# Twelve attention outputs transposed by VectorE squares and a DRAM trip in place of TensorE, with decays scanned in place

## The chip, the cores and the metric

The kernel runs on one core of a Trainium2 chip. The metric is the device time in microseconds (us) of one execution, taken as a median over runs. The engines of the core are named as the profile names them: PE is TensorE (PEld is its weight load), DVE is VectorE, ACT is ScalarE, POOL is GpSimd, and SP is the engine whose queue issues nearly all DMAs here.

## The reference, cut to what matters

A gated linear attention (4 batches, 8 heads, 768 positions, head size 40) is followed by two feed-forward layers over its 3072 tokens of width 320, each with 2048 hidden units. All data is 32-bit float.

```python
# attention, per batch and head, over positions t
C = f_stab * C + i_stab * outer(v_t, k_t);  n = f_stab * n + i_stab * k_t
y[:, :, t] = sigmoid(o_gate_t) * (C @ q_t) / max(abs(n @ q_t), 1)
# then, with the heads side by side as x of [3072, 320]
h = x @ w_in;   x = (h - tanh(h)) @ w_out                 # layer 0
h = x @ w2_in;  g = h if h >= 1, 0 if h <= -1, else (h + 1)**2 / 4
out = g @ w2_out                                          # layer 1
```

## The kernel before, in words

**Tokens and blocks.** The positions of each batch are cut in 6 chunks of 128. One chunk of one batch, with all its 8 heads, is a *job*; there are 24, numbered 0 to 23 (job n is chunk n // 4 of batch n % 4). Four jobs make a *block* of 512 tokens. Layer 0 of block k needs the attention outputs of its four jobs, 4k to 4k + 3.

**Steps.** Each layer goes over 6 blocks of 16 *steps*. A step of layer 0 takes 128 of the 2048 hidden units: 8 matmuls of 512 columns into a PSUM bank `h` (`step`, line 650), then on ACT a tanh (line 668) and a rounded copy `gh` (line 681), on DVE a subtraction (line 669) and the rest `gl` (line 682), and two steps later 12 matmuls of 320 columns into the four `a` banks (`second`, line 702). Two `h` banks are in turn. From block 2 on the steps go in pairs: 16 matmuls of line 650, then 24 of line 702. After 16 steps `evac` has VectorE turn the four `a` banks in squares of 32 by 32 (line 713) and stores them to DRAM (`xr_d`), from where layer 1 loads them in place.

**Jobs beside steps.** The jobs of block k + 1 run while layer 0 of block k runs. A job loads its inputs; scans the decays on DVE (line 460, `fb` in, `d` out); forms the scores on PE (lines 473 and 489), multiplies them into `d` on DVE (line 493), and sums on PE into the bank `t_n`: from the state `C` (line 520), and from scores and values (line 529). Then come a denominator (lines 536 to 539) and the output gate `o3`, a part of the tile `nat`. Line 546 (DVE) multiplies `t_n` and `o3` into the tile `x`, with 128 tokens on the partitions and 320 features along them. Layer 0 wants it the other way round: line 551 has PE transpose `x` in three pieces into a PSUM bank `t_x`, and `split_x` (lines 597 to 607) writes from that bank a rounded part (ACT) and the rest (DVE) into the `x1` tile of the block, which the matmuls of line 650 read. The state is renewed by matmuls of line 558, five copies on ACT and three updates on DVE (line 575).

**What sets the order.** The whole program is first recorded: `op` notes an operation with its engine, an assumed duration and a due time in steps (`prio`). `schedule` then places operations by due time and readiness, and `issue` writes the instructions of each engine in that order. On the chip each engine works strictly in order, and so does SP's queue: a DMA whose wait is not over holds up all behind it. A job of block k ≥ 1 gets its due times from line 816: 6 steps (`AHEAD`) before its share of the block before, its loads 3 steps earlier still. At every chunk the gates (`gates`, `decays`) of all batches are computed, which takes exponentials (line 365) and then sigmoids (line 504) on ACT, with a table load for each. `background` converts a weight tile of layer 1 every four steps and stores it to DRAM (`w_d`). Buffer numbers are the last argument of `abuf`: before, `fb` has 2 and `d` has 3.

Of the kernel before, what the change touches and what calls it, by code (L numbers as in the profile page):

```python
# [7 lines left out]
F32 = mybir.dt.float32  # L8
# [6 lines left out]
ALU = mybir.AluOpType  # L15
PSUM = bass.MemoryType.PSUM

B, H, S, D = 4, 8, 768, 40
L = 128
NC = S // L  # L20
DM = H * D
DF = 2048
NF = DF // 128
# [3 lines left out]
HU = H // 2  # L27
# [5 lines left out]
BLK = [4, 4, 4, 4, 4, 4]  # L33
NB = len(BLK)
BLK0 = [sum(BLK[:j]) for j in range(NB)]
NJ = B * NC
# [9 lines left out]
AHEAD, LOADS = 6, 3  # L46
# [7 lines left out]
W_AHEAD = 5  # L54
FFN = 4
STACK = 12
GS = 4
HTAGS = ["h", "h", "tn", "tb"]

# [16 lines left out]
class Plan:  # L76
# [20 lines left out]
    def op(self, eng, ns, prio, fn, r=(), w=(), out=None, lock=False):  # L97
        o = Op()
        o.eng, o.ns, o.prio, o.fn, o.seq, o.out = eng, ns, prio, fn, len(self.ops), out
        o.allocs, o.preds, o.succs = [], set(), []  # L100
        o.bufs, o.fill, o.lock = [], 0, lock
        key = lambda x: x if isinstance(x, tuple) else (x, None)

        for x in map(key, r):
            if x in self.last:
                o.preds.add(self.last[x])
            self.read.setdefault(x, []).append(o)
        for x in map(key, w):
            if x in self.last:
                o.preds.add(self.last[x])  # L110
            o.preds.update(self.read.pop(x, ()))
            self.last[x] = o
        o.preds.discard(o)
        for b in {key(x)[0] for x in (*r, *w)}:
            if isinstance(b, Buf):
                b.users.append(o)
                o.bufs.append(b)
        if any(b.place[0].startswith("late_") for b in o.bufs):
            o.preds.add(self.gate)
        self.ops.append(o)  # L120
        return o
# [92 lines left out]
def dve(n):  # L214
    return 157 + n / 0.96
# [16 lines left out]
def mlstm_moe_moe(ctx: ExitStack, tc: tile.TileContext, ig, fg, qk, qk3, q3, nat, w1, w2, cst, out):  # L232
    nc = tc.nc
# [5 lines left out]
    dram = ctx.enter_context(tc.tile_pool(name="dram", bufs=1, space=bass.MemoryType.DRAM))  # L239
# [11 lines left out]
    gr_d = dram.tile([B * H, S], F32, name="gr_d")  # L251
    w2_d = dram.tile([NF, 128, WC], F32, name="w2_d")
    xr_d = dram.tile([DM, NT], F32, name="xr_d")

    att = ExitStack()
    ap = att.enter_context(tc.tile_pool(name="ap", bufs=1))
# [10 lines left out]
    def abuf(tag, shape, dtype, cap, name=None):  # L267
        att_tags.add(tag)
        return P.buf(of(ap), shape, dtype, tag, name or tag, cap)
# [12 lines left out]
    def load(prio, dst, src, kb, r=(), w=(), rows=None, eng="SP"):  # L282

        size = rows or 4096
        ns = kb * 1024 / size / 16 * (8 + size / 18.0)
        op(eng, 0, prio, lambda: (nc.sync if eng == "SP" else nc.scalar).dma_start(out=dst(), in_=src()), r, w, out=ns)
# [108 lines left out]
    def jbank(n, what, name):  # L395

        tag = {"s0": "tn", "s1": "tb", "n": "tn", "x": "tn", "c": "tb", "f": "h"}[what]
        if n < FIRST and what in "s0s1xc":
            tag = (("a3", "tb"), ("a0", "a1"))[n % 2][what in ("s1", "x")]
        return bank(tag, name)  # L400
# [5 lines left out]
    def job(n, at, ld):  # L406
# [15 lines left out]
        f = {}  # L422
        if n >= FIRST:
            for u in range(2):
                ft = abuf("fb", [128, HU, L], F32, 2)
                load(ld + 0.5, lambda ft=ft: ft.t, lambda u=u: fr_d[
                    b * H + u * HU:b * H + (u + 1) * HU, c * L:(c + 1) * L].unsqueeze(0).to_broadcast([128, HU, L]),
                    256, r=[("fr_d", kc)], w=[ft], rows=512)
                f[u] = lambda ft=ft: ft.t.rearrange("p h t -> p (h t)"), ft
# [15 lines left out]
        for u in range(2):  # L445
            p = at(0) if u == 0 else at(1)
            if n < FIRST:
                ft = jbank(n, "f", "t_f")
                for h in range(HU):
                    r = b * H + u * HU + h  # L450
                    op("PE", 2 * pe(L, 128, 2), p, lambda h=h, r=r, ft=ft: nc.tensor.matmul(  # L451
                        ft[:, h * L:(h + 1) * L], ident[:, r:r + 1].to_broadcast([128, 128]),
                        gt[0][0][:, 0:L], start=True, stop=True), [gt[0][0], (gt[0][0], "z", 32), (gt[0][0], "z", 64), "cs"], [ft])
                f[u] = lambda ft=ft: ft.t, ft
            if d0 is None:
                d = abuf("d", [128, 512], F32, 3)
                dk[u] = lambda d=d: d.t, d
            else:
                dk[u] = lambda u=u: d0[:, u * 512:(u + 1) * 512], (d0, u)
            op("DVE", dve(1024), p, lambda o=dk[u][0], i=f[u][0]: nc.vector.tensor_tensor_scan(  # L460
                out=o(), data0=i(), data1=scan_id, initial=0.0, op0=ALU.mult, op1=ALU.add), [f[u][1], "scan_id"], [dk[u][1]], lock=n >= FIRST)
            if not last:
                op("ACT", 200, p + 0.3, lambda u=u, i=dk[u][0]: nc.scalar.copy(  # L463
                    wc[:, u * HU:(u + 1) * HU], i().rearrange("p (h t) -> p h t", t=L)[:, :, L - 1]), [dk[u][1]], [(wc, u)])
# [77 lines left out]
        if not xt:  # L542
            xt.append(abuf("x", [128, 384], F32, 1))
            op("POOL", 170, -80, lambda: nc.gpsimd.memset(xt[0][:, DM:384], 0.0), [], [(xt[0], "z")])
        x = xt[0]
        op("DVE", dve(DM), at(6), lambda: nc.vector.tensor_tensor(
            out=x[:, 0:DM].rearrange("p (h e) -> p h e", e=D), in0=pn()[:, :, 0:D],
            in1=o3().rearrange("p (h e) -> p h e", e=D), op=ALU.mult), [p, O], [x])
        px = jbank(n, "x", "t_x")
        for k in range(3):  # L550
            op("PE", pe(128), at(7), lambda k=k: nc.tensor.transpose(  # L551
                px[:, k * L:(k + 1) * L], x[:, k * 128:(k + 1) * 128], ident), [x, (x, "z"), "cs"], [px])

# [32 lines left out]
        if k == 0:  # L586
            op("ACT", act(384), at(8), lambda: nc.scalar.copy(
                xf[0][:, :, z], px[:, 0:384].rearrange("p (k t) -> p k t", k=3)), [px], [(xf[0], n)])
            if n == BLK[0] - 1:
                a = xf[0]  # L590
                split_x(x1[0, 0], slice(0, BLK[0] * L), lambda: a[:, 0:2, 0:BLK[0] * L], lambda: a[0:64, 2, 0:BLK[0] * L],
                        [(a, m) for m in range(BLK[0])], "DVE", WIDE - 4, "x", BLK[0] * L, True)
        else:
            split_x(x1[0, k], z, lambda: px[:, 0:256].rearrange("p (k t) -> p k t", k=2), lambda: px[0:64, 256:384],
                    [px], "DVE", at(8), n, L)
# [211 lines left out]
    def jobs(k):  # L807
        for i, (a, _) in enumerate(GROUPS):
            if i and a * B == BLK0[k]:
                gates(i, GATES[i])  # L810
                decays(i, DECAYS[i])
        for n in range(BLK0[k], BLK0[k] + BLK[k]):
            if k == 0:
                job(n, lambda s: JOB0 + JOBD * n + JOBS * s, LOAD[n])
            else:
                st = NF * (k - 1) + NF * (n - BLK0[k]) / BLK[k] - AHEAD
                job(n, lambda s: st + s, st - LOADS)

    jobs(0)
# [113 lines left out]
```

## Time and profile before

| What | Value |
|---|---|
| median of 3 runs (lowest to highest) | 812.14 us (809.82 to 814.26) |
| the profiled execution | 814.0 us |
| its span, first to last instruction | 812.2 us |
| PE busy | 800.9 us, 99% |
| DVE, ACT, POOL busy | 564.3, 428.2, 149.9 us |
| granted TensorE clock | 1.000, the 2.4 GHz level all through |
| DMA | 93.66 MB, mean 115 GB/s |

The first 33 us prepare the first block, layer 0 then takes until about 463 us, and layer 1 the rest. PE's busy time overstates its load, since a matmul's shown span overlaps the next; the pace from one start to the next tells more. A wait row names the engine, the line that waited, what ended the wait, and the total, the count and the longest.

### The profile page before, as it was taken

What the parts mean: (1) busy time and instruction counts of PE and PEld (TensorE: products, weight loads), DVE (VectorE), ACT (ScalarE), POOL (GpSimd) and SP (SyncE); (2) the same over time, 40 slices, a digit from 0 to 9 for tenths busy, and PEclk for the clock granted to TensorE, in tenths of its full rate; (3) what the DMA queues carried; (4) which work ended last, traced back from release to release, by engine and by line L of the source; (5) the groups of instructions that cost most, each with busy time, mean ns of one, the idle gap of its engine ahead of it and who ended that gap; (6) DMA issues with size and microseconds to landing.
All of it is one profiled execution on the core that took longest, in us unless ns stands there. A gap on an engine that the chain in (4) does not pass through costs nothing.

```text
span 812.2 us, 15272 instructions
## 1 busy us (share of the span) xinstructions
PE 800.9 (99%) x6030; PEld 693.5 (85%) x6034; DVE 564.3 (69%) x922; ACT 428.2 (53%) x810; POOL 149.9 (18%) x147
## 2 busy tenths in 40 slices
PE   8999999999999999999999999999999999999998
PEld 6666888888898989998999888898888889898887
DVE  6899989878888987887556684554646555564644
ACT  4866775675676677645354552443524435342432
POOL 3233122314323333342010200200200201000000
PEclk9999999999999999999999999999999999999999
DMA  8899367686768776871353220100100000000000
GB/s 289 284 259 280 103 192 170 161 255 151 206 189 230 197 201 188 232 191 60 95 163 107 54 71 1 40 33 1 40 33 1 33 1 1 33 1 2 33 1 32
DMA packets 62980, 93.66 MB, mean 115 GB/s; under 512 B 4701, under 2 KB 45501, under 8 KB 62909
## 3 DMA queue, kind: packets, MB, share of 16 engines
q1 hardware_dynamic: 62860, 92.66, 39.3%
q8 instruction: 47, 0.77, 0.5%
q14 instruction: 25, 0.20, 0.1%
q10 hardware_dynamic: 48, 0.03, 0.0%
HBM read 78.88 MB, written 13.80 MB: 114 GB/s over the span
## 4 chain that ended last, share of the span: by engine, by line
PE 93%; DVE 3%; DMA 1%; issue 1%; ACT 1%; POOL 0%; SPq 0%; POOLq 0%; DVEq 0%; ACTq 0%
PE a L702 40%; PE h L650 37%; PE h L640 3%; PE t_n L529 2%; PE h L629 2%; PE t_s L473 2%; PE t_n L520 1%; PE t_c L558 1%; PE spare L796 1%; PE t_x L551 1%; PE t_s L489 1%; PE t_f L451 1%; DMA gb<-gr_d 1%; DVE d L460 1%; DVE w L322 1%
## 5 line engine op out<-in xcount | busy, mean ns | idle before, releaser
L650 PE MATMUL h<-x,w 128*128 128x512 f32 x1376 | 342.3, 396 | 0.0
L702 PE MATMUL a<-w,gh 128*128 128x320 f32 x1472 | 329.7, 310 | 0.0
L650 PEld LDWEIGHTS h<-x,w 128*128 128x128 f32 x1376 | 250.9, 188 | 54.4 <-issue 6.9
L702 PEld LDWEIGHTS a<-w,gh 128*128 128x128 f32 x1472 | 249.2, 188 | 8.5 <-ACT ob L725 1.8
L702 PE MATMUL a<-w,gl 128*128 128x320 f32 x736 | 228.2, 310 | 0.0
L673 DVE TENSOR_SCALAR g<-h 128x512 f32<-128x512 f32 x96 | 63.7, 684 | 115.9 <-PE h L650 115.9
L675 ACT ACTIVATE g<-g,half 128x512 f32<-128x512 f32 x96 | 67.0, 721 | 136.2 <-DVE g L673 135.4
L702 PEld LDWEIGHTS a<-w,gl 128*128 128x128 f32 x736 | 138.2, 188 | 0.5
L669 DVE TENSOR_TENSOR h<-h,g 128x512 f32<-128x512 f32 x88 | 61.0, 694 | 35.8 <-ACT g L668 35.4
L677 DVE TENSOR_TENSOR g<-h,g 128x512 f32<-128x512 f32 x96 | 64.6, 692 | 27.6 <-ACT g L675 26.7
L681 ACT CAST gh<-g 128x512 fp32r<-128x512 f32 x96 | 59.4, 622 | 43.2 <-DVE g L677 42.3
L766 POOL TENSOR_TENSOR x<-xl,x 128x512 fp32r<-128x512 f32 x18 | 24.8, 1402 | 275.3 <-ACT x L757 275.3
L682 DVE TENSOR_TENSOR gl<-h,gh 128x512 fp32r<-128x512 f32 x88 | 60.3, 685 | 21.4 <-ACT gh L681 20.5
L668 ACT ACTIVATE g<-h 128x512 f32<-128x512 f32 x88 | 52.6, 598 | 41.9 <-PE h L650 41.7
L681 ACT CAST gh<-h 128x512 fp32r<-128x512 f32 x88 | 51.4, 584 | 41.1 <-DVE h L669 27.1
L682 DVE TENSOR_TENSOR gl<-g,gh 128x512 fp32r<-128x512 f32 x96 | 61.9, 686 | 3.2 <-ACT gh L681 0.4
L460 DVE TENSOR_TENSOR_SCAN d<-fb,scan_id 128x512 f32<-128x512 f32 x40 | 53.6, 1348 | 1.7 <-DMA fb<-fr_d 1.5
L486 POOL TENSOR_TENSOR xf<-qkraw,xf 120x1024 fp32r<-120x1024 f32 x12 | 30.3, 2523 | 57.8 <-ACT wc L463 12.3
L484 ACT ACTIVATE xf<-qkraw,cs 120x512 fp32r<-120x512 f32 x48 | 32.7, 718 | 14.9 <-PE t_s L489 14.6
L539 POOL TENSOR_TENSOR nat<-nat,dn 128x320 f32<-128x320 f32 x24 | 23.2, 968 | 65.4 <-DVE dn L538 65.4
L493 DVE TENSOR_TENSOR d<-t_s,d 128x512 f32<-128x512 f32 x48 | 31.7, 679 | 3.3 <-PE t_s L489 2.5
L500 POOL TENSOR_TENSOR nat<-nat,isT 128x328 f32<-128x328 f32 x24 | 20.3, 858 | 65.0 <-DVE isT L372 20.0
(103 smaller groups left out, 765.5 us busy)
## 6 DMA issues: line engine op xcount, KB each, us to landing
w<-in_w_dram SPq DMA_DIRECT2D x32, 703.6 KB
nat<-in_nat_dram SPq DMA_DIRECT2D x24, 484.0 KB
qkraw<-in_qk_dram SPq DMA_DIRECT2D x24, 480.0 KB
fb<-fr_d SPq DMA_DIRECT2D x40, 256.0 KB
w_d<-w SPq DMA_DIRECT2D x16, 352.0 KB
w<-w_d SPq DMA_DIRECT2D x16, 352.0 KB
qkraw<-in_qk_dram SPq DMA_DIRECT2D x24, 160.0 KB
xr_d<-xo SPq DMA_DIRECT2D x24, 160.0 KB
```

The lines of the kernel that those rows point to most:

```text
L460: op("DVE", dve(1024), p, lambda o=dk[u][0], i=f[u][0]: nc.vector.tensor_tensor_scan(out=o(), data0=i(), data1=scan_id, initial=0.0, op0=A ...
L484: op("ACT", act(512, 1), at(u - 1), lambda raw=raw, t=t, z=z, cols=cols: nc.scalar.activation(t[:, cols], raw[:, cols], AF.Copy, scale=cs[ ...
L493: op("DVE", dve(512), at(2 + u), lambda p=sp[u], d=dk[u][0]: nc.vector.tensor_tensor(out=d(), in0=p.t, in1=d(), op=ALU.mult), [sp[u], dk[u ...
L650: op("PE", pe(n), prio, lambda i=i, c=c, s=s: nc.tensor.matmul(p[:, :n], w[:, c:c + 128], x[:, s, :n], start=(i == 0 and not layer), stop= ...
L668: op("ACT", act(n), prio + 0.5 - FFN, lambda: nc.scalar.activation(t[:, :n], p[:, :n], AF.Tanh), [p], [t])
L669: op("DVE", dve(n), prio + 0.5 - FFN, lambda: nc.vector.tensor_tensor(out=p[:, :n], in0=p[:, :n], in1=t[:, :n], op=ALU.subtract), [p, t], [p])
L673: op("DVE", dve(n), prio + 0.5 - FFN, lambda: nc.vector.tensor_scalar(t[:, :n], p[:, :n], -1.0, 1.0, op0=ALU.max, op1=ALU.min), [p], [t])
L675: op("ACT", act(n, 1), prio + 0.5 - FFN, lambda: nc.scalar.activation(t[:, :n], t[:, :n], AF.Square, bias=half[:, 0:1], scale=0.5), [t, "h ...
L677: op("DVE", dve(n), prio + 0.5 - FFN, lambda: nc.vector.tensor_tensor(out=t[:, :n], in0=p[:, :n], in1=t[:, :n], op=ALU.max), [p, t], [t])
L681: op("ACT", act(n), prio + 1 - FFN, lambda: nc.scalar.copy(gh[:, :n], y[:, :n]), [y], [gh])
L682: op("DVE", dve(n), prio + 1 - FFN, lambda: nc.vector.tensor_tensor(out=gl[:, :n], in0=y[:, :n], in1=gh[:, :n].bitcast(F32), op=ALU.subtra ...
L702: op("PE", pe(DM) if gl is not None else 2 * pe(DM, 128, 2), prio, lambda A=A, r=r, a=a, c=c, i=i, dt=dt: nc.tensor.matmul(A[:, 0:DM], a[: ...
```

## The change

Jobs 12 to 23 (`TURN = 12`) no longer use line 551 nor a `t_x` bank. For them line 546 writes in place into `o3`. VectorE then turns the 128 by 320 output in squares of 32 by 32 into `x`; four DMAs store the four partition quarters to a DRAM tile `xa_d`, each so that rows of 32 values (128 bytes) fall in their place of the transposed matrix; two DMAs load it back into a tile `xa` with features on the partitions, and `split_x` reads that SBUF tile. The due times of these jobs and of their loads move 4 steps ahead (`TRIP = 4`). In all jobs from 4 on the scan of the decays writes over its input: `fb` has 4 buffers, and `d` is gone. Lines after 57 move down in the changed file: 546 is 549 there, 650 is 665, 702 is 717.

```diff
+TURN, TRIP = 12, 4
...
+    xa_d = dram.tile([NJ, DM, L], F32, name="xa_d")
...
-                ft = abuf("fb", [128, HU, L], F32, 2)
+                ft = abuf("fb", [128, HU, L], F32, 4)
...
             if d0 is None:
-                d = abuf("d", [128, 512], F32, 3)
-                dk[u] = lambda d=d: d.t, d
+                dk[u] = f[u]
...
-        op("DVE", dve(DM), at(6), lambda: nc.vector.tensor_tensor(
-            out=x[:, 0:DM].rearrange("p (h e) -> p h e", e=D), in0=pn()[:, :, 0:D],
-            in1=o3().rearrange("p (h e) -> p h e", e=D), op=ALU.mult), [p, O], [x])
-        px = jbank(n, "x", "t_x")
-        for k in range(3):
+        turn = n >= TURN
+        to = (lambda: o3()) if turn else (lambda: x[:, 0:DM])
+        op("DVE", dve(DM), at(6), lambda to=to: nc.vector.tensor_tensor(
+            out=to().rearrange("p (h e) -> p h e", e=D), in0=pn()[:, :, 0:D],
+            in1=o3().rearrange("p (h e) -> p h e", e=D), op=ALU.mult), [p, O], [O if turn else x])
+        if turn:
+            op("DVE", dve(DM), at(6.5), lambda: nc.vector.transpose(
+                x[:, 0:DM].rearrange("p (j r) -> p j r", r=32), o3().rearrange("p (j i) -> p j i", i=32)), [O], [x])
+            for z in range(4):
+                load(at(6.6), lambda z=z: xa_d[n, :, z * 32:z * 32 + 32].rearrange("(j i) r -> i j r", i=32),
+                     lambda z=z: x[z * 32:z * 32 + 32, 0:DM].rearrange("p (j r) -> p j r", r=32), 40, [x], [("xa_d", n, z)], rows=128)
+            xl = abuf("xa", [128, 3, L], F32, 1)
+            back = [("xa_d", n, z) for z in range(4)]
+            load(at(6.7), lambda: xl[:, 0:2], lambda: xa_d[n, 0:256].rearrange("(m p) t -> p m t", p=128), 128, back, [(xl, 0)], rows=512)
+            load(at(6.7), lambda: xl[0:64, 2], lambda: xa_d[n, 256:DM], 32, back, [(xl, 1)], rows=512)
+        px = None if turn else jbank(n, "x", "t_x")
+        for k in range(0 if turn else 3):
...
+        elif turn:
+            split_x(x1[0, k], z, lambda: xl[:, 0:2], lambda: xl[0:64, 2], [(xl, 0), (xl, 1)], "DVE", at(8), n, L, True)
...
-                st = NF * (k - 1) + NF * (n - BLK0[k]) / BLK[k] - AHEAD
+                st = NF * (k - 1) + NF * (n - BLK0[k]) / BLK[k] - AHEAD - (TRIP if n >= TURN else 0)
```

The first place is PE at the end of job 18, in block 3: before, the state matmuls `t_c`, half a step, the three transposes, the other half (from `h` to `a`).

```order
L702 MATMUL a<-w_1897,gh 128x320 x2
L702 MATMUL a<-w_1897,gl 128x320
L558 MATMUL t_c<-nat 120x123 x2
L558 MATMUL t_c<-nat 80x82
L650 MATMUL h<-x_2605,w_955 128x512 x4
L551 MATMUL t_x<-cs,x 128x128 x3
L650 MATMUL h<-x_2605,w_955 128x512 x4
L650 MATMUL h<-x_2605,w_996 128x512 x8
```

The same job's end on PE in the changed program:

```order
L490 MATMUL t_s<-xf 128x128 x4
L665 MATMUL h<-x_2715,w_1819 128x512 x6
L571 MATMUL t_c<-nat 120x123
L530 MATMUL t_n<-nat,fb 32x41 x32
L571 MATMUL t_c<-nat 120x123
L571 MATMUL t_c<-nat 80x82
L665 MATMUL h<-x_2715,w_1819 128x512 x2
L665 MATMUL h<-x_2715,w_1871 128x512 x8
L717 MATMUL a<-w_1689,gh 128x320 x2
```

The transposes are gone, the steps' matmuls stand in one row, and the job's other matmuls stand closer together.

The second place is SP's queue around the trip of job 17, the one with the shortest way, in the changed program (`xa_d<-x` are the stores, `xa<-xa_d` the loads back).

```order
L288 DMA xa_d<-x 32x10x32 x4
L288 DMA nat<-in_nat_dram 128x968
L288 DMA q_3551<-in_q_dram 120x384
L288 DMA qkraw<-in_qk_dram 120x1024
L288 DMA xa<-xa_d 128x2x128
L288 DMA gb<-gr_d 40x3x128 x2
L288 DMA gb<-gr_d 40x2x128
L288 DMA xa<-xa_d 64x128
```

Before, the loads of `nat`, `gb` and `q` follow each other with nothing between that waits for a store.

```order
L286 DMA xr_d<-xo 32x10x128 x4
L286 DMA nat<-in_nat_dram 128x968
L286 DMA gb<-gr_d 40x3x128 x2
L286 DMA gb<-gr_d 40x2x128
L286 DMA q_3662<-in_q_dram 120x384
```

Now three loads stand between the stores and the first load back, and four DMAs of the next jobs stand behind a load that waits for the stores.

The third place is ACT at the gates of chunk 4, some 41 steps into layer 0, in the changed program. The first exponential of the chunk, with its table load, stands just ahead; then follow the table load for the sigmoids (line 505), the state copies (`t_c`), the split of a job that comes back (`x_2715<-xa`), the next tanh, and a second table load for the exponentials (line 367).

```order
L505 ACT_TABLE_LOAD
L505 ACTIVATE nat<-nat 128x320
L579 ACTIVATE t_c<-t_c,cs 120x2x41
L583 ACTIVATE t_c<-t_c,cs 80x41
L579 ACTIVATE t_c<-t_c,cs 120x2x41
L583 ACTIVATE t_c<-t_c,cs 80x41
L579 ACTIVATE t_c<-t_c,cs 120x2x41
L616 CAST x_2715<-xa 128x2x128
L620 CAST x_2715<-xa 64x128
L683 ACTIVATE g<-h 128x512
L367 ACT_TABLE_LOAD
L367 ACTIVATE ig<-ig 32x128
```

Before, the same gates read so, with one load of each kind per chunk:

```order
L365 ACT_TABLE_LOAD
L365 ACTIVATE fr<-fr 32x128
L681 CAST gh<-h 128x512
L536 ACTIVATE t_n<-t_n 128x8
L365 ACTIVATE ig<-ig 32x128
```

A sigmoid has come between the two exponentials of this chunk, so that the program holds 12 table loads where it held 10.

## Rows read from the trace of the kernel before

**Rows 1.** The profile's page: busy times, granted clock, chain that ended last, DMA queue.

```profile
PE 800.9 (99%) x6030; PEld 693.5 (85%) x6034; DVE 564.3 (69%) x922; ACT 428.2 (53%) x810; POOL 149.9 (18%) x147
PEclk9999999999999999999999999999999999999999
PE 93%; DVE 3%; DMA 1%; issue 1%; ACT 1%; POOL 0%; SPq 0%; POOLq 0%; DVEq 0%; ACTq 0%
q1 hardware_dynamic: 62860, 92.66, 39.3%
```

**Rows 2.** Busy by stretch: length, then PE, PEld, DVE, ACT, POOL (instructions), clock, DMA.

```profile
133.10:227.10 94.00, 90.96 (x858) 80.40 (x858) 78.55 (x136) 58.85 (x128) 28.21 (x28) 1.00 0.71 191
191.90:227.10 35.20, 34.78 (x327) 31.18 (x326) 30.57 (x50) 19.67 (x47) 12.63 (x11) 1.00 0.64 170
264.10:336.60 72.50, 72.50 (x676) 65.25 (x674) 60.81 (x105) 46.43 (x100) 26.36 (x24) 1.00 0.72 202
336.60:405.30 68.70, 68.70 (x641) 61.84 (x641) 49.03 (x77) 33.50 (x63) 19.45 (x17) 1.00 0.46 128
```

**Rows 3.** The same for line 650 alone, 128 matmuls being 16 steps.

```profile
264.10:336.60 72.50, 33.48 (x129) 22.88 (x129) 1.00 0.72 202
```

**Rows 4.** Timeline of PE at transposes: start, us, instruction, idle before it.

```profile
310.26 1.17 PE L650 MATMUL h<-x,w 128*128 128x512 f32 x4
311.27 0.49 PE L551 MATMUL t_x<-cs,x 128*128 128x128 f32 x3
311.52 0.48 PE L650 MATMUL h<-x,w 128*128 128x512 f32 x1
...
220.02 0.52 PE L551 MATMUL t_x<-cs,x 128*128 128x128 f32 x3 [0.42 <-ACT t_c L570]
...
259.65 0.52 PE L551 MATMUL t_x<-cs,x 128*128 128x128 f32 x3 [0.19 <-DVE x L546]
```

**Rows 5.** Groups by line: count | busy us, mean ns | idle before, and its enders.

```profile
L551 PE MATMUL t_x<-cs,x 128*128 128x128 f32 x72 | 12.0, 275 | 2.0 <-DVE x L546 1.4 <-ACT t_c L570 0.4
L713 DVE STREAM_TRANSPOSE xo<-a 128x320 f32<-128x320 f32 x24 | 10.7, 487 | 1.3 <-PE a L702 1.3
L460 DVE TENSOR_TENSOR_SCAN d<-fb,scan_id 128x512 f32<-128x512 f32 x40 | 53.6, 1348 | 1.7 <-DMA fb<-fr_d 1.5
L493 DVE TENSOR_TENSOR d<-t_s,d 128x512 f32<-128x512 f32 x48 | 31.7, 679 | 3.3 <-PE t_s L489 2.5
L486 DVE TENSOR_TENSOR xf<-qkraw,xf 120x1024 fp32r<-120x1024 f32 x12 | 15.7, 1309 | 1.0 <-ACT xf L484 0.7
L365 ACT ACT_TABLE_LOAD x5 | 6.4, 1283 | 1.3 <-PEq L920 1.2
```

**Rows 6.** Issues on SP's queue and what came after: timeline, and chain of waits.

```profile
347.13 2.40 SPq L286 DMA_DIRECT2D xr_d<-xo  x4
...
172.08 3.49 DMA fr_d<-fr
...
178.96 6.10 DMA gb<-gr_d
...
356.48 0.36 SPq L286 DMA_DIRECT2D q<-in_q_dram  x1
...
359.26 0.75 POOL L510 TENSOR_TENSOR q<-q,gb 120x256 f32<-120x256 f32 x1 [1.34 <-DMA q<-in_q_dram]
```

**Rows 7.** Who waited, 191.9 to 405.3 us: total, times, longest.

```profile
ACT g L668 <- PE h L650: 23.7, 26, 3.2
PE t_x L551 <- ACT t_c L570: 0.4, 1, 0.4
PE t_x L551 <- DVE x L546: 0.2, 1, 0.2
```

## The prediction

> **What bounds the kernel now.** The page comes first: PE is busy 99% of the span and makes up 93% of the chain that ended last, its clock is granted in full in all 40 slices, and DVE, the next engine, is busy 69% [rows 1]. So the time is PE's work plus PE's pauses, and the change counts where it alters one of the two. Second, the stretches of layer 0 in which jobs 12 to 23 run, 191.9 to 405.3 us: PE has hardly a gap there, while DVE is busy 87%, 84% and 71% of the first, the middle and the last stretch shown [rows 2]. DVE has room, but little before 264 us. Third, the pace: 128 matmuls of line 650, which are 16 steps, with four jobs take 72.5 us [rows 3], 4.5 us a step. By that I turn distances in the program's order into time. Fourth, the waits: in that stretch PE stood still for DVE or ACT at a transpose for 0.6 us only [rows 7]. Most of what there is to win is PE work, not pauses.
>
> **The transposes that go.** The group row gives 275 ns for one piece [rows 5], and 36 pieces would be 9.9 us. That is too much, since shown spans of matmuls overlap. The timeline tells what they hold up: three pieces start at 311.27 and the next matmul of line 650 at 311.52 [rows 4], 0.25 us for a job. Twelve jobs give **-3.0 us**, and since PE is saturated all of it lies on the path. The two pauses at transposes, 0.42 and 0.19 us [rows 4], end because ACT and DVE catch up; without the transposes PE meets the same late engines at the next `h` bank. I take half, **-0.3**, out of 0 to -0.6.
>
> A page of the Trainium skill speaks against this exchange: VectorE: DVE Perf Modes, section Rules for kernel authors, has a 128 by 128 transpose done by TensorE wherever a PSUM destination will do. Here PSUM does, and by that rule these 3.3 us would better not be bought with DVE and DMA work; the rows decide otherwise only because PE is at 99% and DVE at 69%.
>
> **DVE's squares, and denser jobs.** A turn of 128 by 320 from PSUM takes 487 ns [rows 5]; twelve are 5.9 us of DVE, beside PE where DVE has gaps. The split keeps its instructions and only reads SBUF, for which I set nothing. But the jobs also close up. Counted in the order, jobs 12, 16 and 20 start no earlier, since they wait for their gates, and jobs 13 to 15 (and so on) follow at distances of 2 to 4 steps and not 4. Between step 20 and step 40 DVE gets one scan more (1.35), two products (2 x 0.68), one split of `xf` (1.31), three squares (3 x 0.49) [rows 5] and smaller pieces, together some 6 us more than before. In that stretch DVE was busy 78.6 of 94.0 us [rows 2], so it would reach 84.6 of 94, 90%. It fits on average, not at each point. If none of it were covered it cost 6 us; but PE does most of one more job there as well, which it then need not do later. I take **+0.5**, out of 0 to +3.
>
> **The trip.** After the square, SP issues four stores, four of which took 2.40 us before (`xr_d`); the last must land, a load be issued, and it must land [rows 6]. For a landing the rows have a short end (2.8 us from the issue of `q` at 356.48 to its reader at 359.26), a store to DRAM in traffic (3.49) and a broadcast load in traffic (6.10) [rows 6]. Short end: three issues at 0.36 ahead of the fourth, 2.8 and 2.8, so 6.7 us. Long end: 2.4, 3.5 and 6.1, so 12.0 us. The order leaves, from the square on DVE to the first split on ACT, for jobs 12 to 23 in steps: 2.5, 2.3, 2.3, 3.7, 2.7, 1.6, 2.3, 5.5, 1.9, 1.9, 2.1, 2.7; at 4.5 us that is from 7.2 (job 17) to 25 us. At the short end no split is late. At the long end eight are, by 20 us summed (4.8 for job 17, 3.4 each for jobs 20 and 21, 2.5 for job 22, 1.6 each for jobs 13, 14 and 18, 0.8 for job 12).
>
> What is queued behind a late split on ACT is the next tanh, and so DVE's subtraction, the `h` bank and PE. The cover is ACT's own waiting: it stood for PE's `h` 26 times in this stretch, 0.9 us on average and 3.2 at most [rows 7]. On SP, four DMAs of the next jobs stand behind the load back in the row shown, and wait as long as the stores need; their buffers are for jobs some steps ahead. Most trips should be nearer the short end, as they lie between the bursts: I take 8.5 us, by which job 17 is late by 1.3 and no other, and set **+0.3**.
>
> **Two table loads more.** 2 x 1.28 us of ACT [rows 5], at the gates of chunk 4. ACT is busy 64% in the stretch from 264 us [rows 2], but the order has the next tanh behind them. Between 0 and 2.6 us; **+0.4**.
>
> **Scans in place.** As many scans of the same size. An `fb` buffer is now held until the sums on PE are done, but two jobs fit in four buffers, so loads are issued earlier than before. The program before block 3 is shuffled by this; PE paused 1.4 us for `x` in the whole trace, nearly all of it before 192 us [rows 5, 7], and such a pause may go or come: 0, out of -1.4 to +1.4.
>
> **Sum.** -3.0 - 0.3 + 0.5 + 0.3 + 0.4 = -2.1 us. The profiled execution took 814.0, which makes 811.9; the median of the runs is 1.9 lower, and on it, 812.14, the forecast is **810.0 us**.
>
> **Rivals.**
> *A, the trip comes late and holds ACT (slower).* For it: ACT is in order, and 8 of 12 distances are below the long end. Against it: layer 0's DMA share is 0.46 in the last stretch [rows 2], and a store waits behind little there. Price: 20 us of ACT waiting, less the 0.9 of cover at each of eight, is 12.8 us on PE; -2.4 from the other terms leaves +10.4, **822.5 us**. It turns slower from a trip of about 10 us on. The stores have a cost that no row shows, since they go in 1280 pieces of 128 bytes for a job. A mean packet held one DMA engine for 0.393 x 16 x 812.2 / 62860 = 0.081 us [rows 1]; 80 such for each engine are 6.5 us, while by bytes alone (160 KB among 1474-byte packets) they are 0.6. In the worst case that makes this rival. The Trainium skill's DMA: Bandwidth & Descriptors, section Specifications, states 512 bytes as the least transfer for the full rate and a read-modify-write below it; by that rule the upper of these ends is the nearer one.
> *B, DVE becomes the bound where jobs close up.* For it: 84 to 87% busy up to 264 us already [rows 2]. Against: it has 9 us of gaps in the stretch that gets 6 more. Price: +3 in place of +0.5, so **812.5 us**.
> *C, the new order also removes pauses.* PE's own work is fixed, but each break between a step's matmuls and a job's costs it something, and denser jobs mean fewer. Against it: PE is without marked gaps from 264 us on [rows 2], so the room is small. With the 0.6 and the 1.4 us of pauses gone and no loss anywhere: -5.0, **807.1 us**.
> *D, it doesn't do what it says.* Excluded by the order: no transposes on PE for jobs 12 to 23.
>
> **How the numbers follow.** Forecast 0.48 (its own range 807 to 814), A 0.16, B 0.12, C 0.24. The range leaves out A's upper half and the far end of C: 804.5 to 817.0. A measurement of this kernel tells about 0.5%, 4.1 us, from no change: 808.1 and 816.2. Below lie C and the lower fifth of the forecast, 0.34; above lie A and a sixth of B, 0.18; within 0.48.
>
> **What would show it.** Right: no transposes after job 11, PE's pace a quarter us shorter per job, twelve squares of about 0.49 us, ACT waiting for `xa` seldom and by under 2 us, and no row of PE waiting in 264 to 405 us. Wrong by A: ACT waiting for a DMA of `xa` in the list of waits by over 10 us in total, and the gap passed on to line 650's successor. Wrong by B: DVE at 95% or more between 133 and 227 us, with PE waiting for it. Layer 1 should take the same time to a tenth of a us per block; if it doesn't, none of this holds.

## The result and the profile after

The changed kernel took 821.9 us (median of 4 runs, 818.9 to 824.6) beside 812.5 for the kernel before on the same chip: a ratio of 1.0118 with a 95% interval of 1.007 to 1.0165. The forecast was a gain, to 810.0 in a range of 804.5 to 817.0; the time lies above that range, and the change cost time. The profiled execution took 818.9 us, the lowest of the four, with a span of 817.1.

The page after, answering [rows 1]: busy times, granted clock, chain that ended last, DMA queue.

```profile
PE 801.1 (98%) x5994; PEld 692.3 (85%) x5998; DVE 573.5 (70%) x934; ACT 430.2 (53%) x812; POOL 147.4 (18%) x147
PEclk9999999999999999999999999999999999999999
PE 75%; DMA 11%; DVE 8%; ACT 3%; issue 2%; SPq 1%; POOL 0%; DVEq 0%; ACTq 0%
q1 hardware_dynamic: 83212, 96.60, 41.6%
```

PE has 36 instructions fewer and is hardly less busy; its share of the chain fell from 93% to 75%. DVE's share of the span rose by one point only. The windows that answer [rows 2], in the same order and columns:

```profile
133.10:227.10 94.00, 90.79 (x902) 79.37 (x900) 80.47 (x138) 59.72 (x131) 31.07 (x31) 0.98 0.79 213
191.90:227.10 35.20, 33.67 (x305) 29.25 (x306) 29.25 (x51) 20.59 (x51) 14.33 (x17) 0.95 0.74 185
264.10:336.60 72.50, 70.52 (x651) 63.38 (x650) 61.03 (x103) 44.67 (x98) 27.16 (x24) 0.98 0.74 196
336.60:405.30 68.70, 68.12 (x628) 60.50 (x627) 56.47 (x89) 33.41 (x64) 16.15 (x15) 1.00 0.66 173
```

PE has gaps now from 191.9 to 336.6 us, and the clock is granted less than in full. DVE's busy share is no higher there (83% in the second window, where it was 87%); in the last window it rose from 71 to 82%, and there PE hardly paused. The pauses stand in PE's timeline:

```profile
192.50 3.58 PE L665 MATMUL h<-x,w 128*128 128x512 f32 x8 [1.76 <-DVE gl L697]
214.90 1.42 PE L665 MATMUL h<-x,w 128*128 128x512 f32 x5 [0.81 <-DVE gl L697]
231.55 0.63 PE L490 MATMUL t_s<-xf 120*128 120x128 f32 x4 [1.36 <-DVE nat L549]
251.97 2.08 PE L665 MATMUL h<-x,w 128*128 128x512 f32 x8 [1.89 <-DVE fr L390]
...
307.98 0.63 PE L490 MATMUL t_s<-xf 120*128 120x128 f32 x4 [1.57 <-DVE nat L549]
```

Each time PE waited for DVE (the row at 251.97 names a memset of 0.06 us that DVE ran right behind `gl`). After the first and the last of these pauses the clock fell to its half level, 1.2 GHz, for 3.4 us. Two windows of 8 us around them show it in the clock's column, 0.79:

```profile
189.00:197.00 8.00, 6.24 (x83) 5.07 (x84) 5.20 (x8) 3.09 (x7) 5.94 (x6) 0.79 0.86 239
305.00:313.00 8.00, 6.43 (x28) 5.27 (x28) 6.46 (x12) 4.69 (x9) 0.46 (x1) 0.79 0.32 62
```

Layer 1 is the same: from its first activation on ACT to the end it took 345.96 us, before 345.97. All of the loss lies in layer 0.

**An account of the span.** A span can be split in three: PE's pauses between 130 and 412 us (each start-to-start interval of PE less the median of its line, where it is over 0.25 us longer), the time lost to the clock (one less the mean clock, times the span, good to 0.4 us), and the rest, which is PE's own pace.

| profiled run | span | pauses | clock | rest |
|---|---|---|---|---|
| before | 812.2 | 5.2 | 0.0 | 807.0 |
| after | 817.1 | 10.9 | 3.3 | 802.9 |

So the gain is there, and larger than forecast: 4.1 us in PE's pace, 0.34 for a job. It went in 5.7 us more of pauses and 3.3 us of clock. The profiled executions took 814.0 and 818.9 us where the medians are 812.5 and 821.9, so the account covers 4.9 of 9.4 us. The clock was at 0.995 or 0.996 in all four executions of the changed kernel, so what its median holds above that execution is not clock; no trace shows where it lies. The experiments ask what made the pauses. The medians below stand beside runs of the kernel before on the same chip (812.97 to 813.66 us). In some runs of most of these kernels the clock was granted in full and in others not; the medians hold both.

### The profile page after: what moved, and what is told of

The parts are those of the page before. It is cut to its first block, busy times and chain, and to the rows that moved or that the text cites. A ratio compares the mean times of both kernels' runs of the same rounds, so it can differ in the third digit from the quotient of the medians.

```text
span 817.1 us, 15326 instructions
## 1 busy us (share of the span) xinstructions
PE 801.1 (98%) x5994; PEld 692.3 (85%) x5998; DVE 573.5 (70%) x934; ACT 430.2 (53%) x812; POOL 147.4 (18%) x147
## 4 chain that ended last, share of the span: by engine, by line
PE 75%; DMA 11%; DVE 8%; ACT 3%; issue 2%; SPq 1%; POOL 0%; DVEq 0%; ACTq 0%
PE a L717 34%; PE h L665 32%; DMA xa<-xa_d 4%; PE h L655 2%; PE h L644 2%; DMA nat<-in_nat_dram 2%; DMA w_d<-w 1%; DVE fb L461 1%; DMA w<-in_w_dram 1%; SPq L288 1%; DMA fr_d<-gate 1%; DVE gl L697 1%; PE t_n L521 1%; PE t_n L530 1%; DVE h L684 1%
## 5 line engine op out<-in xcount | busy, mean ns | idle before, releaser
L461 DVE TENSOR_TENSOR_SCAN fb<-fb,scan_id 128x512 f32<-128x512 f32 x40 | 55.4, 1392 | 0.3 <-DMA fb<-fr_d 0.2
L322 ACT ACTIVATE cvb<-w,half 128x704 bf16<-128x704 int8 x32 | 30.1, 940 | 7.2 <-DVE w L324 4.5
L511 POOL TENSOR_TENSOR q<-q,gb 120x256 f32<-120x256 f32 x20 | 18.2, 908 | 80.6 <-DMA q<-in_q_dram 39.2
```

## The experiments

**The parts alone.** Three kernels take one part each: scans in place alone, the trip without the lead of four steps, and the lead without the trip.

```diff
-TURN, TRIP = 12, 4
+TURN, TRIP = 24, 4        # e1_inplace
+TURN, TRIP = 12, 0        # e2_trip0
```

```diff
-TURN, TRIP = 12, 4        # e3_shift
+TURN, TRIP = 24, 4
-                st = NF * (k - 1) + NF * (n - BLK0[k]) / BLK[k] - AHEAD - (TRIP if n >= TURN else 0)
+                st = NF * (k - 1) + NF * (n - BLK0[k]) / BLK[k] - AHEAD - (TRIP if n >= 12 else 0)
```

> Only the scans in place and the four fb buffers; all 24 jobs keep TensorE's transposes and their due times. If the scans in place matter (a third theory), this is slower than before by 3 us or more; by the two main theories (the trip holds ACT; the earlier due times crowd DVE) it stays within 2.5 us of before, 810 to 815 us, with PE pauses of some 5 us or less in layer 0.

Measured 0.9995 (0.9977 to 1.0013). The scans in place are free.

> The whole change but the earlier due times (TRIP = 0): squares and trip, jobs four steps apart. If crowding (the shift) costs the time, the pauses of PE shrink to under 4 us, its clock stays granted in full, and the time falls to 809 to 814 us. If the trip holds ACT, ACT waits for xa by 8 us or more as in the changed kernel and the time stays at 818 to 824 us.

Measured 1.0095 (1.0065 to 1.0125). ACT waited 4.8 us for the trip, under the 8 that the second theory wanted. Without the lead PE waits at the starts of blocks 3 and 4 for the split of the last job, 2.1 and 2.6 us, as the changed kernel does not; the two ratios can't be told apart.

> The scans in place and the due times of jobs 12 to 23 four steps ahead, but TensorE's transposes kept, so no squares and no trip. If crowding costs the time, it is at 817 to 824 us, with PE pauses of 2 us in layer 0. If the trip does, it is within 3 us of before, 810 to 815.5 us.

Measured 1.0043 (1.0027 to 1.0058), between the two ranges. The lead alone, with the transposes kept, costs 3.5 us in this order.

**What the transposes are worth.** One kernel issues them twice; two leave them out together with squares and trip and let the split read the untransposed `x`, without the lead and with it.

```diff
-        for k in range(0 if turn else 3):
+        for k in [*range(3)] * (2 if n >= 12 else 1):        # e5_double
+        for k in range(0 if n >= 12 else 3):                 # e6_direct, e9_shiftdirect
...
+        elif n >= 12:
+            split_x(x1[0, k], z, lambda: x[:, 0:256].rearrange("p (k t) -> p k t", k=2), lambda: x[0:64, 256:384],
+                    [x, (x, "z")], "DVE", at(8), n, L, True)
```

> Scans in place only, no trip; the three transposes of each of jobs 12 to 23 are issued twice, into the same bank. My term (a job's three transposes hold up PE by 0.25 us, and PE is saturated): 12 x 0.25 = 3.0 us more than before, ratio about 1.0037, PE's busy row longer by about that. Rival 1, the transposes lie in time that PE has to spare: ratio 1.000. Rival 2, the durations of the group row count in full (36 x 0.275 us): 9.9 us, ratio 1.012.

Measured 1.0061 (1.0048 to 1.0074), 5.0 us or 0.41 for a job, and a rest of 811.1 in the account. My term was too small, the full sum of the group row's durations too large.

> Scans in place, no transposes for jobs 12 to 23, no squares, no trip, no shift of due times: the split reads the token-major tile x in SBUF as it stands, so the features and tokens of these jobs are not the attention's. It keeps the whole gain and drops every cost but the read from SBUF. Theory (transposes are worth 3.0 us, and 0.6 us of pauses at them): ratio 0.9956 to 0.9963, 809.5 to 810.0 us on a before of 813. Rival, the DVE half of the split is what hurts, because it reads SBUF beside GpSimd (0.47 us per job, 5.6 us in all): the split stays long (over 0.6 us) and the ratio is 0.999 to 1.003.

Measured 0.9960 (0.9943 to 0.9977), 3.3 us faster: the gain is real, and two more table loads, which this order holds too, do not spoil it. The split's pieces are long here too (560 and 582 ns in the mean), and it costs little. The longest, 2.55 us, began with a subtraction on GpSimd; PE meanwhile worked through matmuls of line 717 and passed from them to those of line 665 without a pause:

```profile
368.38 2.41 POOL L487 TENSOR_TENSOR xf<-qkraw,xf 120x1024 fp32r<-120x1024 f32 x1 [0.28 <-ACT t_n L537]
368.40 2.55 DVE L621 TENSOR_TENSOR x<-x,x 64x128 fp32r<-64x128 f32 x1
...
370.69 4.25 PE L665 MATMUL h<-x,w 128*128 128x512 f32 x16
```

> The same (no transposes, no squares, no trip, token-major split), with the due times of jobs 12 to 23 moved 4 steps ahead as in the change. Theory (shift alone costs 0.43%, transposes give 0.40%): ratio 1.000, between 0.998 and 1.002, and more by 0.0035 to 0.005 than the run without the shift. Rival, the price of the shift was the chance of one order and not the crowding of jobs on DVE: the ratio is that of the run without the shift, 0.996 to 0.997.

Measured 0.9971 (0.9956 to 0.9985). Here the lead costs 0.1%, which is within the noise, and not 0.43%: its price hangs on the order around it.

**The trip.** One kernel keeps the changed order and takes only the wait for the stores away; the other lets the planner know that the trip is longer, so that the splits stand later.

```diff
-            load(at(6.7), lambda: xl[0:64, 2], lambda: xa_d[n, 256:DM], 32, back, [(xl, 1)], rows=512)
+            load(at(6.7), lambda: xl[0:64, 2], lambda: nat[b, 256:DM, 0:L], 32, back, [(xl, 1)], rows=512)   # e4_nowait, and the first load likewise
+            load(at(6.7), lambda: xl[0:64, 2], lambda: xa_d[n, 256:DM], 32, back, [(xl, 1)], rows=512).more = 6000.0   # e7_know, likewise
...
-                o.end = dma + self.DMA_OUT
+                o.end = dma + self.DMA_OUT + o.more          # e7_know
```

> The changed kernel instruction for instruction, but the loads into xa read an input of the same shape and not xa_d, so they don't wait for the stores (the values of jobs 12 to 23 are therefore not the attention's). The stores stay. If the trip holds ACT, its waits for xa fall from 10 us to under 3 us, the pauses of PE behind them (at 213.7, 229.9, 249.8 us) go, and the time is 812 to 816 us. If crowding costs the time, it stays at 818 to 824 us.

Measured 1.0041 (1.0019 to 1.0063). ACT still waited 8.7 us for the loads themselves, so this run does not take the wait away, and its time lies between the two ranges.

> The change as it is, but the planner is told that a load back of the trip lands 6 us later than it assumed, so that the splits on ACT stand further behind the squares (3.5 to 4.2 steps in place of 1.6 to 2.7, most of them), and 10 table loads are left. Theory (ACT held by the wait for the trip costs about 6 us): ACT waits for the trip under 2 us in total, ratio 1.000 to 1.005. Rival (the crowding on DVE costs it, and the wait only shows where it ends): ACT waits no longer, and the ratio stays at 1.008 to 1.012.

Measured 1.0025 (1.0006 to 1.0044). ACT did not wait for the trip at all. But the DVE half of the split also became short again, and nothing was done to it. Means of the two pieces of the split on DVE in this kernel, and then in the changed one (count, busy us, mean ns, idle before):

```profile
L618 DVE TENSOR_TENSOR x<-xa,x 128x256 fp32r<-128x256 f32 x12 | 5.3, 442 | 0.7 <-ACT x L617 0.7
L622 DVE TENSOR_TENSOR x<-xa,x 64x128 fp32r<-64x128 f32 x12 | 3.4, 285 | 0.4
```

```profile
L617 DVE TENSOR_TENSOR x<-xa,x 128x256 fp32r<-128x256 f32 x12 | 8.0, 668 | 6.1 <-ACT x L616 6.1
L621 DVE TENSOR_TENSOR x<-xa,x 64x128 fp32r<-64x128 f32 x12 | 6.0, 499 | 0.3
```

From the PSUM bank `t_x` the same pieces take 417 and 284 ns.

**Squares and DMAs alone.** To see which of them costs the 0.54% between the last two ratios (0.9971 and 1.0025), each was added by itself to the kernel with lead and direct split.

```diff
+        turn = n >= 12                     # e10_squares: product into nat, square into x, split from x, no DMAs
...
+        if n >= 12:                        # e11_traffic: the four stores of x and two loads into xa, which nobody reads
```

> The run with the shift and the direct split, plus DVE's twelve squares (product in place into nat, turned into x, split read from x); still no stores and no loads back, so these jobs' values are not the attention's. Between the direct split with the shift (ratio 0.9971) and the trip that the planner knows of (1.0025) lie 4.4 us, for squares and DMAs together. Theory S, DVE is the scarce one: the squares cost most of it, ratio 1.000 to 1.002. Rival D, the DMAs and their latency cost it: ratio 0.996 to 0.998.

Measured 1.0067 (1.0043 to 1.0091).

> The run with the shift and the direct split, plus the six DMAs of each trip (four stores in 128-byte rows, two loads back into a tile that nothing reads), no squares; the split waits for none of them, but the next job's product waits until the stores have read x, and four DMAs queue behind each load back. Theory S (the squares cost the 4.4 us): ratio 0.996 to 0.998. Rival D (queueing and traffic cost it): 1.000 to 1.002, with scans waiting for their decays' load by over 3 us in total.

Measured 1.0050 (1.0033 to 1.0068). Both expectations fell: each alone came out dearer than both together (for the DMAs the intervals overlap). The timeline of the kernel with squares alone tells why (start, us, instruction, idle before):

```profile
206.58 2.37 POOL L487 TENSOR_TENSOR xf<-qkraw,xf 120x1024 fp32r<-120x1024 f32 x1 [1.78 <-ACT xf L485]
206.59 2.50 DVE L620 TENSOR_TENSOR x<-x,x 64x128 fp32r<-64x128 f32 x1
...
210.96 0.64 DVE L696 TENSOR_TENSOR gl<-h,gh 128x512 fp32r<-128x512 f32 x1
211.66 0.73 PE L664 MATMUL h<-x,w 128*128 128x512 f32 x2 [3.37 <-DVE gl L696]
```

A piece of 0.29 us took 2.50, as long as GpSimd's subtraction that began with it; `gl` came late and PE stood 3.4 us. The kernel with DMAs alone has the same meeting at 206.10 (2.52 us) and a pause of 2.1 us. So these two ratios hold the price of a meeting that their orders happen to have, and not that of squares or DMAs alone. Such a meeting costs where PE soon needs what DVE has behind it; in the kernel at 0.9960 it did not.

**The causes taken away in one order.** The next kernels keep the order of their parent instruction for instruction, and leave out a part of the computation. One lets the split read a constant tile, so that nothing waits for the trip; one cuts GpSimd's subtraction to 64 of 1024 columns; one does both; and the same cut is made in the kernel with squares alone and, as a control, in the kernel before.

```diff
-            split_x(x1[0, k], z, lambda: xl[:, 0:2], lambda: xl[0:64, 2], [(xl, 0), (xl, 1)], "DVE", at(8), n, L, True)
+            split_x(x1[0, k], z, lambda: scan_id[:, 0:256].rearrange("p (k t) -> p k t", k=2), lambda: scan_id[0:64, 256:384],
+                    [(xl, 0), (xl, 1)], "DVE", at(8), n, L, True)        # e13_cut, e19_cut_pool
...
-                    out=t.t, in0=raw.t, in1=t.t.bitcast(F32), op=ALU.subtract), [raw, t], [t], eng="POOL" if u == 0 else "DVE")
+                    out=t[:, 0:m], in0=raw[:, 0:m], in1=t[:, 0:m].bitcast(F32), op=ALU.subtract), [raw, t], [t], eng="POOL" if u == 0 else "DVE")   # m = 64 on GpSimd: e14_pool and the other _pool kernels
```

> The changed kernel instruction for instruction in the same order, squares, stores and loads back included, but the split of jobs 12 to 23 reads a constant tile in SBUF in place of the one that comes back, so nothing waits for the trip (and these jobs' values are left out of layer 0). Theory (a), ACT held by the trip: no pause of PE near 230, 250 and 306 us, no stretch at half clock there, ratio 1.000 to 1.004. Rival (c), the denser jobs and squares cost it themselves: ratio 1.006 or more, pauses at the same places for DVE.

Measured 1.0051 (1.0031 to 1.0072), between the two. ACT's waits are gone, the split pieces stay long (670 and 634 ns), and the pause at 191 us stays (1.7 us, the clock at half behind it).

> The changed kernel in the same order, trip included, but GpSimd's subtraction for xf (2.4 to 3.3 us each, twelve times) takes 64 of its 1024 columns, so the scores of those jobs are not exact. Theory (b), DVE and GpSimd hinder each other at SBUF and that makes DVE late: the scan mean falls from 1392 to under 1300 ns, the DVE half of the split from 668 to under 450 ns, the pauses of PE near 190 and 306 us go, ratio 1.003 to 1.008. Rival (a), ACT held by the trip sets it alone: DVE's rows fall, PE's pauses after ACT's waits stay, ratio 1.009 to 1.013.

Measured 1.0051 (1.0030 to 1.0072). The trip still holds ACT for 9.8 us, the split's large piece is down to 412 ns and the scans to 1274, and the pause at 190 us is gone:

```profile
L461 DVE TENSOR_TENSOR_SCAN fb<-fb,scan_id 128x512 f32<-128x512 f32 x40 | 50.6, 1274 | 0.9 <-DMA fb<-fr_d 0.8
L621 DVE TENSOR_TENSOR x<-xa,x 64x128 fp32r<-64x128 f32 x12 | 5.1, 428 | 0.3
L617 DVE TENSOR_TENSOR x<-xa,x 128x256 fp32r<-128x256 f32 x12 | 4.9, 412 | 7.1 <-ACT x L616 7.1
```

> The changed kernel's order, with both suspected causes removed: the split reads a constant tile and never waits for the trip, and GpSimd's subtraction takes 64 of 1024 columns. If the two explain the loss: ratio 0.996 to 0.999 (the gain on PE less what is left in pauses), PE's pauses in layer 0 back to 5 us or fewer. If the denser jobs cost by themselves: 1.001 or more.

Measured 0.9973 (0.9957 to 0.9989). With both away the kernel is faster than before. PE's pauses came to 6.1 us in the account, above the 5 that were expected.

> The run with shift, direct split and squares (1.0067), same order, with GpSimd's subtraction cut to 64 columns. If its price was the collision (one split piece took 2.50 us in place of 0.29 beside GpSimd, and PE then stood 3.5 us): ratio 0.996 to 0.999. If the squares themselves crowd DVE: 1.003 to 1.006.

Measured 0.9941 (0.9918 to 0.9963), below both ranges, where the parent had 1.0067.

> Control: the kernel before, same order, with GpSimd's subtraction for xf cut to 64 of its 1024 columns. In the trace of before DVE's scan takes 1215 ns alone and up to 2079 beside GpSimd, but its split reads PSUM and keeps its time. If the collision is the change's own: ratio 0.998 to 1.000, scan mean under 1290 ns and no more. If GpSimd's work costs every version the same: 0.993 to 0.995.

Measured 0.9988 (0.9972 to 1.0005): the same cut is worth 0.1% in the kernel before, 0.67% in the changed one, 0.78% in it without the trip's wait, and 1.26% with squares alone. The scan's mean is 1296 ns, just above the 1290 that were expected. So it is no general gain from less GpSimd work. (The cut also lets `xf` be ready some 2 us earlier. The control has that too; what it is worth where jobs are denser was not tried by itself.)

**Versions.** Three more ask whether a smaller dose pays, all with the longer trip known to the planner: jobs 20 to 23, jobs 16 to 23, and all twelve with a lead of two steps (`TURN, TRIP = 20, 4`, `16, 4` and `12, 2`).

> The change for jobs 20 to 23 only, with the planner told that the load back lands 6 us later. Gain 4 x 0.3 = 1.2 us. If squares and trip cost only where DVE has no room (it is 71% busy in this stretch), ratio 0.998 to 0.999; if they cost the same 0.37 us at every job, 1.0003 to 1.0005.

> The same for jobs 16 to 23, most of which lie behind 264 us, where DVE is busy 84 and 71%. Gain 8 x 0.3 = 2.4 us. If the cost lies with jobs 12 to 15, where DVE is busy 87% and more: ratio 0.997 to 0.998. If it is even over the jobs: 1.001 to 1.002.

> The change with the planner told that the load back lands 6 us later, and the jobs 2 steps ahead in place of 4. If the denser jobs cost what is left (1.0025 at 4 steps): 0.999 to 1.001. If the lead is needed, PE waits at the starts of blocks for the split of the last job, as with no lead at all: 1.004 to 1.009.

Measured 1.0004 (0.9987 to 1.0021), 1.0007 (0.9989 to 1.0025) and 1.0051 (1.0031 to 1.0071). The first two can't be told from no change. With two steps of lead PE waits 3.1 us for the split at a block's start. No version with the trip that computes the whole result beat the kernel before.

## Why the forecast was wrong, point by point

**The account over all runs.** The rest of the span is 806.7 to 807.3 us in the four kernels with the transposes, 811.1 with them doubled, and 802.4 to 804.7 in the thirteen that leave out all twelve. So PE's own pace is 2.0 to 4.9 us shorter in every kernel without these transposes; what else sets these spans is pauses (3.1 to 13.3 us) and clock (0 to 4.1 us).

**Transposes, -3.0.** Right in kind, too small: -4.1 in the account, 0.34 us a job. The reading in [rows 4] took the delay of the next start alone, 0.25 us. In the same trace the matmul after that one starts 0.32 us later, where 0.23 is usual; with that the three cost 0.34. The -0.3 for pauses at transposes can't be told in a trace with 10.9 us of pauses.

**"The split keeps its instructions and only reads SBUF, for which I set nothing."** This is the first step that failed, and with it the term for denser jobs, which took DVE's durations from group means. Taking GpSimd's part away in the same order gave back 0.67% (1.0118 to 1.0051, intervals that just touch) or 5.4 us, and 0.78% (1.0051 to 0.9973) where nothing waits for the trip. That is the price for the split and for the scans together; no run divides it. What it is shows in the changed kernel at 188 us:

```profile
188.39 2.39 POOL L487 TENSOR_TENSOR xf<-qkraw,xf 120x1024 fp32r<-120x1024 f32 x1 [0.15 <-ACT xf L485]
188.99 2.87 DVE L461 TENSOR_TENSOR_SCAN fb<-fb,scan_id 128x512 f32<-128x512 f32 x1
191.78 0.66 DVE L697 TENSOR_TENSOR gl<-h,gh 128x512 fp32r<-128x512 f32 x1
```

and at 300 us, in the split itself:

```profile
298.75 3.30 POOL L487 TENSOR_TENSOR xf<-qkraw,xf 120x1024 fp32r<-120x1024 f32 x1 [7.99 <-ACT xf L485]
300.08 0.41 ACT L616 CAST x<-xa 128x256 fp32r<-128x256 f32 x1 [1.46 <-DMA xa<-xa_d]
300.51 1.82 DVE L617 TENSOR_TENSOR x<-xa,x 128x256 fp32r<-128x256 f32 x1 [0.73 <-ACT x L616]
302.36 0.71 DVE L621 TENSOR_TENSOR x<-xa,x 64x128 fp32r<-64x128 f32 x1
```

The kernel before has the same at single scans: here one alone, and then one that began while GpSimd's subtraction ran, with `gl` between.

```profile
319.90 1.22 DVE L460 TENSOR_TENSOR_SCAN d<-fb,scan_id 128x512 f32<-128x512 f32 x1
...
360.78 2.93 POOL L486 TENSOR_TENSOR xf<-qkraw,xf 120x1024 fp32r<-120x1024 f32 x1 [0.36 <-ACT t_n L536]
362.00 0.69 DVE L682 TENSOR_TENSOR gl<-h,gh 128x512 fp32r<-128x512 f32 x1 [0.44 <-ACT gh L681]
362.72 2.08 DVE L460 TENSOR_TENSOR_SCAN d<-fb,scan_id 128x512 f32<-128x512 f32 x1
```

In the changed kernel a scan of 1.21 us takes 2.87 and a piece of 0.42 takes 1.82; they end 1.1 and 0.3 us after GpSimd's subtraction, as the piece of 0.29 in the kernel with squares alone ended 0.1 us after it. The Trainium skill's page SBUF — State Buffer, section Who interferes with whom, has the rule: a DVE instruction with two SBUF inputs contends with a GpSimd instruction that reads SBUF, and the order of issue decides which of them waits. The traces agree: in the kernel before, the scan (two SBUF inputs) takes 1.21 us alone and up to 2.08 beside GpSimd, while `gl` (one input in PSUM) keeps to 0.69 either way. Moving the split's source from PSUM to SBUF gave both its pieces a second SBUF input: with GpSimd idle they still take 0.42 and 0.29 us, beside it up to 1.82 and 1.12. And the lead moved scans under GpSimd: the kernel with the lead alone (1.0043), whose split reads PSUM, has a scan of 2.70 us at 191.42 and a pause of 1.58 behind it. The mean of 1348 ns for the scan in [rows 5] held this already; I read it as a duration and not as two.

**The trip, +0.3.** The second step that failed: "Most trips should be nearer the short end". Job 12's trip, on SP's queue and at its ends:

```profile
199.90 0.49 DVE L553 STREAM_TRANSPOSE x<-nat 128x320 f32<-128x320 f32 x1
200.41 0.33 SPq L288 DMA_DIRECT2D xa_d<-x  x1
...
201.76 1.38 SPq L288 DMA_DIRECT2D xa_d<-x  x3
...
205.55 0.94 SPq L288 DMA_DIRECT2D xa<-xa_d  x2
...
210.83 0.41 ACT L616 CAST x<-xa 128x256 fp32r<-128x256 f32 x1 [1.58 <-DMA xa<-xa_d]
```

It took 10.9 us from square to split, near my long end of 12.0, where I took 8.5. In the eight jobs whose split waited it was 7.9 to 19.3 us. The longest is job 19's: its loads back were issued 9.9 us after its stores, behind fourteen other DMAs of SP's queue, a time that my ends leave out. The small pieces were not the price: a 128-byte packet took 13 ns in the mean, 1.05 us for each DMA engine and job, near the lower of rival A's two ends (0.6 and 6.5). Who waited, in the stretch of [rows 7]:

```profile
ACT x L616 <- DMA xa<-xa_d: 9.2, 8, 2.2
DVE x L617 <- ACT x L616: 6.1, 7, 2.4
PE t_s L490 <- DVE nat L549: 3.6, 4, 1.6
...
ACT x L620 <- DMA xa<-xa_d: 0.9, 1, 0.9
```

Nine waits, 10.1 us: rival A's count of late splits (eight of twelve, six of them the jobs it named) and its sign (over 10 us) were right. In one order taking the wait away gave 0.67% or 5.4 us, half of what ACT waited, where A had 12.8; with GpSimd's subtraction cut it gave 0.78%. Waiting is no measure of the price by itself: the kernel whose loads do not wait for the stores keeps 8.7 us of it at 1.0041. The chain is as A said, with one link more: DVE stood for ACT's half of the split, and then `gl`, the product in `nat` and the next scores were late, for which PE stood.

**The two together.** Removed singly, 0.67% each; together 1.45% (1.0118 to 0.9973). Within the noise they add (the 1.0118 rests on four executions, from 1.007 to 1.0165). What is left, 0.9973, makes 809.9 us of the forecast's 812.14, with 0.1% owed to the control's gain: about the forecast's 810.0. With terms of 5.4 in place of 0.3 and of nothing the sum would have given some 820 us. So A's number, 822.5, came near the result by the wrong sum: half of its loss is another mechanism's.

**Squares, denser jobs, +0.5; B.** Twelve squares came at 508 ns, 21 more than forecast. With GpSimd's subtraction cut the kernel that has them is at 0.9941, so they cost little; no run without them has the same cut. B's sign, DVE at 95%, never came: 86% in 133 to 227 us. The 9 us of gaps that the prediction names there are those left after its 6 us more (94.0 less 84.6); DVE's busy time rose by 1.9 us. DVE was late at single points and not full.

**Table loads, +0.4; scans in place, 0.** The scans are not seen (0.9995). A kernel with twelve loads reached 0.9960, but in the changed order one of the two stands in the way: the chain ahead of the pause at 251.97 runs from the late split through a table load of 1.28 us to a late tanh. With the trip's wait and GpSimd's part both taken away (0.9973) the pause is still there, at 1.08 us:

```profile
245.18 1.28 ACT L367 ACT_TABLE_LOAD   x1
...
247.51 0.57 ACT L683 ACTIVATE g<-h 128x512 f32<-128x512 f32 x1
248.12 0.70 DVE L684 TENSOR_TENSOR h<-h,g 128x512 f32<-128x512 f32 x1 [1.11 <-ACT g L683]
249.46 0.74 PE L665 MATMUL h<-x,w 128*128 128x512 f32 x2 [1.08 <-DVE fr L390]
```

No run takes the load alone away, so its share in this pause is argued and not shown.

**The clock, no term.** The 3.3 us had no place in the sum. The profile before does not show it: its longest wait of PE between 130 and 412 us is 1.2 us, and the clock is granted in full throughout. The 3.3 us came right behind two pauses that were not foreseen.

**Still open.** What the lead costs by itself: 0.43% with the transposes and 0.1% without them, the first with a pause of 2.7 us for `xf` whose cause was not taken apart. And why the kernel whose planner knows the trip stays at 1.0025: neither cause is left in its split, and squares and DMAs cost next to nothing in the changed order once both are away (0.9973, with all of them still there). But its scans still meet GpSimd (1420 ns in the mean), and behind one of them PE stands 1.72 us:

```profile
187.17 2.38 POOL L488 TENSOR_TENSOR xf<-qkraw,xf 120x1024 fp32r<-120x1024 f32 x1
187.79 2.84 DVE L462 TENSOR_TENSOR_SCAN fb<-fb,scan_id 128x512 f32<-128x512 f32 x1
...
191.27 0.96 PE L666 MATMUL h<-x,w 128*128 128x512 f32 x3 [1.72 <-DVE gl L698]
```

PE also stands 1.0 to 1.4 us for ACT's state copies, for `xf` and for `q` near 277, 322 and 341 us. This order was not run with GpSimd's subtraction cut. Its traced execution took 811.7 us and its median is 815.4, so what the median holds more is not shown.

## What to carry to other kernels

Before moving an operand from PSUM to SBUF, split the mean of DVE's two-input instructions into those beside GpSimd and those alone, and ask whom the moved one will meet and what PE has in hand meanwhile; a busy share doesn't show it. A DRAM round trip inserted in an order that is planned must be planned with the time that traffic gives it (here 7.9 to 19.3 us from square to split where the split waited, the time in the queue included), or it holds the in-order engine that consumes it. When several small edits give ratios that do not add, compare kernels of the same order, with one cause taken away by its data.

## What the runs showed of the hardware

A 64 by 128 subtraction on DVE took 0.29 us alone and 2.50 beside a GpSimd subtraction of 2.37 us. After pauses of PE of 1.76 and 1.57 us the granted clock was at 1.2 GHz for 3.4 us, about 1.7 us lost each time; after one of 1.89 us in the same run (at 251.97), after one of 1.72 at the first place in the kernel whose planner knows the trip, and after one of 3.37 in the kernel with squares alone, it stayed at 2.4 GHz. A pause of this size may bring it or not.
